# The second expert product turned round: 128 tokens of g held in the array, 512 columns of w_out streamed, the odd half blocks of two chunks joined

## The chip, the cores and the metric

The kernel runs on one core of a Trainium2 chip. The metric is the device time of one execution in microseconds (us). The reported time is a median of several runs; a profiled execution of the same kernel gives the trace, whose span runs from the first to the last instruction.

## What is computed

The reference is attention with a top-32 mask over 4 batches, 8 heads, 576 tokens and 64 columns a head, followed by a gated product of experts on 2304 tokens. Cut to what matters:

```python
scores = q @ k.T / 8                                  # per batch and head
mask = scores >= (32nd largest of each row)
attn = softmax(where(mask, scores, -1e9))
x = (attn @ v), heads side by side                    # 2304 x 512
a = x @ w_a; b = x @ w_b                              # 512 -> 1536
return (a * b) @ w_out                                # 1536 -> 512
```

The last line is the product that is changed. The letter g stands for a * b below.

## The kernel before

**Chunks and tiles.** The 576 tokens of each batch are cut into a chunk of 256 (`LO`) and one of 320 (`HI`). There are eight chunks, numbered 0 to 7 in the order of the work; their lengths are 256, 320, 256, 320, 256, 320, 320, 256. Attention goes through a chunk by four pairs of heads and, within a pair, by tiles of 64 tokens: 16 tiles for a chunk of 256, 20 for one of 320, 144 in all. For a tile, TensorE makes the scores (L430), VectorE finds the largest 32 of every row in rounds of MAX8 and MATCH_REPLACE8 (L458, L460), ScalarE, GpSimd or VectorE mask and exponentiate, TensorE transposes (L512). After the last tile of a pair, `av` multiplies by v (L540) and splits the result x into a high and a low part, `xh` and `xl` (L543, L544). A chunk's x is complete when the `xl` of its fourth pair is written.

**Experts.** `up(c, j, which)` (j from 0 to 11, which 0 or 1 for w_a and w_b) adds up 12 matmuls in a PSUM buffer of the tag `mm` (L570 to L572: high by high, high by low, low by high, four times). It needs the whole x of its chunk. The copy of the first product (L579) is multiplied by the second (L584, or L587 and L588 in chunks 0 and 1); g is split into `gh` (L589, ScalarE) and `gl` (L590, GpSimd), buffers that hold all twelve j of one chunk, one of each. `down(c, m)` makes the second product for 128 of the 512 output columns: per j three matmuls, L600 to L602, that hold 128 columns of w_out (`fin[j]`) in the array and stream the chunk's 256 or 320 tokens of gh or gl. Four blocks m, each of 36 matmuls, make a chunk. A block ends in a ScalarE copy out of PSUM (L606) and a store on SP's queue (L607) into an output that lies by columns of w_out, and which the host turns round at the end.

**The order of the work.** Every operation is enlisted in a `Plan` with its engine, its estimated cost, a key, and what it reads and writes. `Plan.order` simulates the engines and writes the order out: each engine, when it is free, takes the operation with the lowest key that is ready and for which a buffer is free. Attention has the keys 0 and up (some of it lower), the experts 1000 and up; what is equal goes by the order of enlisting. There are two `mm` buffers, which `up`, `down` and `av` share. Only while none of them is held, and TensorE would be idle, the plan puts in fillers: matmuls with zeros (L288). In the order of enlisting all ups of a chunk stand ahead of its downs. Each unit of `down` waits in the plan for all twelve gh and gl of its chunk:

```python
for j in range(NJ):
    pe(3 * n, lambda j=j: product(j), [(fin[j], 0), (fin[j], 1)] + [(y, k) for y in (gh, gl) for k in range(NJ)], [ps], num=3)
```

The weights come to the kernel in another format and are converted in the first 213 us (`convert`: L384 to L392), w_out last, j from 0 to 11. The ups of chunk 0 run over the j from 7 to 11 and then from 0 to 6; those of odd chunks after chunk 1 run over the j downward, so that the last ones are the small j. From tile 36 on (`COUPLED`) the scores of two tiles are made together, and the first copies and minima of the odd one get a key that is lower by `SOON`.

Of the kernel before, what the change touches and what calls it, by code (L numbers as in the profile page):

```python
# [8 lines left out]
FT = mybir.dt.float32  # L9
FR = mybir.dt.float32r  # L10
# [9 lines left out]
LOW = -3.0e38  # L20
LO, HI = 256, 320
W_BUFS = 8
COUPLED, SOON = 36, 2.5
KEEP = 1
GRP = 2

# [5 lines left out]
CONV_BIG = 4  # L32
# [219 lines left out]
def attn_moe(ctx: ExitStack, tc, qT, kT, v, wa, wb, wo, out):  # L252
# [19 lines left out]

    chunks = [(b, *x) for b in range(B) for x in ([(0, LO), (LO, HI)] if b < B - 1 else [(LO, HI), (0, LO)])]
    pairs = [(c, p) for c in range(len(chunks)) for p in range(NP)]
    tiles = []
    for c, p in pairs:
# [11 lines left out]
    def buf(shape, dtype, tag, bufs, pool=work):  # L290
        return Buf(pool, shape, dtype, tag, bufs)
# [53 lines left out]
    def convert(j, i):  # L345

        src = wo[j] if i == 2 else (wa, wb)[i][j].rearrange("p k e -> p (k e)")  # L350
        n = 2 * NJ + j if i == 2 else 2 * j + i
        if i == 2 and j in CONV_AWAY:
            raw, both = [buf([128, 1024], U4, "w", W_BUFS) for _ in range(2)]
            tmp, low = Part(both, 0, 512), Part(both, 512, 512)
            plan.enlist(raw, both)
        elif n < CONV_FIRST and n % CONV_BIG == CONV_BIG - 1:
            big = buf([128, 3840], U4, ("gh", "gl")[n // CONV_BIG % 2], 1)
            raw, tmp, low = [Part(big, *x) for x in ((0, 1024), (1024, 512), (1536, 512))]
        else:
            while i == 2 and len(listed) + 1 + 2 * sum(x not in CONV_AWAY for x in range(len(listed), j + 1)) > NJ:  # L360
                plan.enlist(fin[len(listed)])
                listed.append(fin[len(listed)])
            raw, both = [buf([128, 1024], U4, "wo", NJ, const) for _ in range(2)]
            tmp, low = Part(both, 0, 512), Part(both, 512, 512)
            plan.enlist(raw, both)
        first = [PR[0]["kr"], PR[0]["qr"]]
        dma(524e3, lambda: nc.sync.dma_start(raw[:, :], src.bitcast(U4)), [], [raw], after=first)
        if i == 2:
            w = fin[j]
            if j == NJ - 1:  # L370
                plan.enlist(*fin)
        else:
            w = buf([128, 2, 4, 128], FR, "w", W_BUFS)

        def word(t):
            return raw[:, :].rearrange("p (n t) -> p n t", t=2)[:, :, t]

        def part(k):
            return w[:, k] if i == 2 else w[:, k].rearrange("p k e -> p (k e)")

        def f(x):
            return x[:, :].bitcast(FT)

        act(512, lambda: nc.scalar.activation(f(tmp), word(1).bitcast(FT), AF.Relu, scale=2.0 ** -116), [raw], [tmp])  # L384
        act(512, lambda: nc.scalar.activation(f(low), word(1).bitcast(FT), AF.Relu, scale=-2.0 ** -84), [raw], [low])
        pool(512, lambda: nc.gpsimd.tensor_tensor(f(tmp), f(tmp), f(low), OP.add), [low], [tmp])
        act(512, lambda: nc.scalar.activation(low[:, :], word(0), AF.Copy, scale=2.0 ** -29 * (1 - 2.0 ** -13),  # L387
                                              bias=7.5 * 2.0 ** -13 - 0.5), [raw], [low])
        dve(0, lambda: vec.scalar_tensor_tensor(tmp[:, :], tmp[:, :], 3, low[:, :], op0=OP.logical_shift_left,
                                                op1=OP.bitwise_or), [low], [tmp], 0.6, port=True)  # L390
        act(512, lambda: nc.scalar.activation(part(0), f(tmp), AF.Copy), [tmp], [(w, 0)])
        pool(512, lambda: nc.gpsimd.tensor_tensor(part(1), f(tmp), part(0).bitcast(FT), OP.subtract), [tmp, (w, 0)], [(w, 1)])  # L392
        if i < 2:
            dma(524e3, lambda: move(wab_d[j][i], w.ap), [(w, 0), (w, 1)], [("wd", j, i)])
        return w
# [149 lines left out]
             [xf, (xh, p)], [(xl, p)])  # L545


    G, A, O = {}, {}, {}

    kept = {}  # L550

    def up(c, j, which, last=False):
        n = chunks[c][2]
        xh, xl = X[c]
        if (c, j, which) in direct:
            w = direct.pop((c, j, which))
            wt = [(w, 0), (w, 1)]
        elif (j, which) in kept:
            w = kept.pop((j, which))
            wt = [w]  # L560
        else:
            w = buf([128, 2, 4, 128], FR, "w", W_BUFS)
            wt = [w]
            dma(524e3, lambda: move(w.ap, wab_d[j][which]), [("wd", j, which)], [w])
        if last and c + 1 < len(chunks):
            kept[j, which] = w
        ps = mm_tile()

        def product(kb):
            mm(ps[:, :n], w[:, 0, kb, :], xh[:, kb, :n], start=(kb == 0), stop=False)  # L570
            mm(ps[:, :n], w[:, 0, kb, :], xl[:, kb, :n], start=False, stop=False)  # L571
            mm(ps[:, :n], w[:, 1, kb, :], xh[:, kb, :n], start=False, stop=(kb == 3))  # L572
        for kb in range(4):
            pe(3 * n, lambda kb=kb: product(kb), wt + [(y, k) for y in (xh, xl) for k in range(NP)], [ps], num=3)
        if which == 0:
            if c not in G:
                G[c] = (buf([128, NJ, HI], FR, "gh", 1), buf([128, NJ, HI], FR, "gl", 1))
            a = A[0] = buf([128, HI], FT, "a", 2)
            act(n, lambda: nc.scalar.activation(a[:, :n], ps[:, :n], AF.Copy, scale=UNIT), [ps], [a], ps=True, k=URGENT)  # L579
            return  # L580
        gh, gl = G[c]
        a = A[0]
        if c >= POOL_PRODUCT:
            dve(n, lambda: vec.scalar_tensor_tensor(a[:, :n], ps[:, :n], UNIT, a[:, :n], op0=OP.mult, op1=OP.mult), [ps], [a], k=URGENT)  # L584
        else:
            y = buf([128, HI], FT, "b", 1)
            act(n, lambda: nc.scalar.activation(y[:, :n], ps[:, :n], AF.Copy, scale=UNIT), [ps], [y], ps=True, k=URGENT)  # L587
            pool(n, lambda: nc.gpsimd.tensor_tensor(a[:, :n], a[:, :n], y[:, :n], OP.mult), [y], [a])  # L588
        act(n, lambda: nc.scalar.activation(gh[:, j, :n], a[:, :n], AF.Copy), [a], [(gh, j)], k=URGENT)  # L589
        pool(n, lambda: nc.gpsimd.tensor_tensor(gl[:, j, :n], a[:, :n], gh[:, j, :n].bitcast(FT), OP.subtract),  # L590
             [a, (gh, j)], [(gl, j)])

    def down(c, m):
        b, t0, n = chunks[c]
        gh, gl = G[c]
        ps = mm_tile()
        ms = slice(128 * m, 128 * m + 128)

        def product(j):
            mm(ps[:, :n], fin[j][:, 0, ms], gh[:, j, :n], start=(j == 0), stop=False)  # L600
            mm(ps[:, :n], fin[j][:, 0, ms], gl[:, j, :n], start=False, stop=False)  # L601
            mm(ps[:, :n], fin[j][:, 1, ms], gh[:, j, :n], start=False, stop=(j == NJ - 1))  # L602
        for j in range(NJ):
            pe(3 * n, lambda j=j: product(j), [(fin[j], 0), (fin[j], 1)] + [(y, k) for y in (gh, gl) for k in range(NJ)], [ps], num=3)
        o = buf([128, HI], FT, "b", 1)
        act(n, lambda: nc.scalar.activation(o[:, :n], ps[:, :n], AF.Copy, scale=UNIT), [ps], [o], ps=True, k=URGENT)  # L606
        dma(512 * n, lambda: nc.sync.dma_start(out[ms, b * S + t0:b * S + t0 + n], o[:, :n]), [o], [])  # L607


    key[0] = -1  # L610
# [3 lines left out]
    for i, t in enumerate(tiles):  # L614
# [38 lines left out]
                for which in range(2):  # L653
                    up(c, j, which, n >= NJ - KEEP)
        key[0] = EXPERTS + c
        for m in range(4):
            down(c, m)


    low, one = buf([128, 3], FT, "low", 1), buf([1, 1], FT, "one", 1)  # L660
# [18 lines left out]
def general(tc, qT, kT, v, wab, wo, ident, out):  # L679
# [7 lines left out]
    with (tc.tile_pool(name="gd", bufs=1, space=bass.MemoryType.DRAM) as dram, tc.tile_pool(name="ga", bufs=2) as sb,  # L687
# [46 lines left out]
        with tc.For_i(0, B, 1) as b:  # L734
            for g in range(2):
# [5 lines left out]
                for j in range(len(wo)):  # L741
                    ab = []
                    for i in range(2):
                        w = sb.tile([128, 2, 4, 128], FR, name="gw")
                        nc.sync.dma_start(w.bitcast(FT), wab[j][i].bitcast(FT))
                        p = ps.tile([128, HS], FT, name="gmm", bufs=2)
                        for kb in range(4):
                            mm(p, w[:, 0, kb, :], xh[:, kb], start=(kb == 0), stop=False)
                            mm(p, w[:, 0, kb, :], xl[:, kb], start=False, stop=False)
# [3 lines left out]
                    nc.vector.tensor_tensor(ab[0], ab[0], ab[1], OP.mult)  # L753
                    nc.scalar.activation(gh[:, j], ab[0], AF.Copy)
                    nc.gpsimd.tensor_tensor(gl[:, j], ab[0], gh[:, j].bitcast(FT), OP.subtract)
                for m in range(4):
                    ms = slice(128 * m, 128 * m + 128)
                    p = ps.tile([128, HS], FT, name="gmm", bufs=2)
                    for j in range(len(wo)):
                        mm(p, wo[j][:, 0, ms], gh[:, j], start=(j == 0), stop=False)  # L760
                        mm(p, wo[j][:, 0, ms], gl[:, j], start=False, stop=False)
                        mm(p, wo[j][:, 1, ms], gh[:, j], start=False, stop=(j == len(wo) - 1))
                    o = sb.tile([128, HS], FT, name="go")
                    nc.scalar.activation(o, p, AF.Copy, scale=UNIT)
                    nc.sync.dma_start(out[ms, ds(b * S + g * HS, HS)], o)


def layout(q, k, v, wa, wb, wo):
# [29 lines left out]
```

## Time and profile before

| | us |
|---|---|
| time, median of 3 runs | 854.4 |
| the 3 runs | 851.25, 854.4, 855.22 |
| profiled execution, its own time | 850.72 |
| its span | 849.0 |
| PE busy in the span | 796.8 (94%) |
| DVE busy | 695.2 (82%) |
| ACT busy | 595.1 (70%) |
| POOL busy | 406.2 (48%) |
| mean granted clock of PE, share of full speed | 0.988 |

PE is TensorE, PEld its weight loads, DVE VectorE, ACT ScalarE, POOL GpSimd, SP the engine that issues the transfers. A matmul's record runs to its modelled end, so the records of matmuls that follow each other overlap; the distance between two starts is what a matmul costs in a stream. A name such as L600 is a line of the kernel. The execution's own time is 1.72 us above its span.

### The profile page before, as it was taken

Reading aid. Unit: us, or ns where it says so; the run is one execution under the profiler, and the core shown is the slowest. Engines: PE = TensorE matmul, PEld = TensorE weight load, DVE = VectorE, ACT = ScalarE, POOL = GpSimd, SP = SyncE. Lnnn points to the kernel's source line nnn. Section 1 sums busy time; section 2 is a strip of 40 time slices with the busy share of each in tenths; the row PEclk is TensorE's granted clock in tenths of the full one; section 3 lists DMA queues with packets and bytes.
Section 4 is the critical chain, followed back from the end, with each engine's and each line's share of the span. In section 5 each row is a group of like instructions: output and inputs, shape, how many; then the busy total and the mean of one; then the engine's idle time right before and its main releaser. Section 6 shows DMA issues by size and latency. Waiting matters only on the chain.

```text
span 849.0 us, 18522 instructions
## 1 busy us (share of the span) xinstructions
PE 796.8 (94%) x6358; PEld 658.0 (77%) x6358; DVE 695.2 (82%) x2240; ACT 595.1 (70%) x1404; POOL 406.2 (48%) x541
## 2 busy tenths in 40 slices
PE   3787889899999999999999999999999999999997
PEld 1444457666888887888888888888888888999997
DVE  4898898988999999999999999999999999710010
ACT  4899988999687777777767777777777777621220
POOL 2677766976357753444444543345344443420120
PEclk8999999999999999999999999999999999999999
DMA  6778748865357732586247741685347721673540
GB/s 204 274 236 274 248 159 285 279 190 173 113 163 237 230 118 60 173 278 211 68 145 232 228 158 61 195 259 191 88 158 225 234 82 39 207 257 122 186 179 29
DMA packets 75430, 153.87 MB, mean 181 GB/s; under 512 B 7232, under 2 KB 46144, under 8 KB 75328
## 3 DMA queue, kind: packets, MB, share of 16 engines
q1 hardware_dynamic: 75328, 152.60, 55.8%
q8 instruction: 53, 0.87, 0.4%
q14 instruction: 49, 0.40, 0.2%
HBM read 135.27 MB, written 17.30 MB: 180 GB/s over the span
## 4 chain that ended last, share of the span: by engine, by line
PE 73%; ACT 11%; DVE 4%; POOL 4%; DMA 3%; issue 2%; SPq 2%; POOLq 0%; DVEq 0%; ACTq 0%
PE mm L570 11%; PE mm L571 10%; PE mm L572 10%; PE tp L512 8%; PE mm L540 8%; PE s L430 8%; PE mm L600 6%; PE mm L601 6%; PE mm L602 6%; ACT p L492 2%; DMA wo<-wa 2%; ACT r L485 1%; DVE mx L460 1%; DVE top L458 1%; ACT wo L387 1%
## 5 line engine op out<-in xcount | busy, mean ns | idle before, releaser
L570 PE MATMUL mm<-xh,w 128*128 128x256 f32 (+1 forms) x768 | 238.0, 310 | 1.0 <-ACT a L579 1.0
L572 PE MATMUL mm<-xh,w 128*128 128x256 f32 (+1 forms) x768 | 227.3, 296 | 0.0
L571 PE MATMUL mm<-xl,w 128*128 128x256 f32 (+1 forms) x768 | 227.2, 296 | 0.0
L458 DVE MAX8 top<-mx 128x8 f32<-128x296 f32 x432 | 187.3, 457 | 1.5
L570 PEld LDWEIGHTS mm<-xh,w 128*128 128x128 f32 x768 | 145.1, 189 | 18.6 <-issue 12.3
L571 PEld LDWEIGHTS mm<-xl,w 128*128 128x128 f32 x768 | 145.4, 189 | 0.0
L572 PEld LDWEIGHTS mm<-xh,w 128*128 128x128 f32 x768 | 144.8, 188 | 0.0
L517 ACT ACTIVATE pt<-tp 128x640 f32<-128x640 f32 x144 | 101.0, 701 | 56.7 <-PE tp L512 55.8
L590 POOL TENSOR_TENSOR gl<-a,gh 128x256 fp32r<-128x256 f32 (+1 forms) x96 | 79.3, 826 | 123.0 <-ACT gh L589 118.9
L460 DVE MATCH_REPLACE8 mx<-top,mx 128x296 f32<-128x296 f32 x288 | 128.7, 450 | 0.0
L499 POOL TENSOR_SCALAR p<-p,sm 128x576 f32<-128x576 f32 x97 | 74.2, 765 | 95.2 <-DVE sm L495 94.8
L600 PE MATMUL mm<-gh,wo 128*128 128x256 f32 (+1 forms) x384 | 119.0, 310 | 0.3 <-ACT b L606 0.2
L512 PE MATMUL tp<-ident,p 128*128 128x128 f32 x720 | 106.3, 279 | 8.3 <-POOL p L499 4.3
L601 PE MATMUL mm<-gl,wo 128*128 128x256 f32 (+1 forms) x384 | 113.6, 296 | 0.4 <-POOL gl L590 0.4
L602 PE MATMUL mm<-gh,wo 128*128 128x256 f32 (+1 forms) x384 | 113.6, 296 | 0.0
L430 PE MATMUL s<-kr,qr 64*64 64x288 f32 x1152 | 92.3, 424 | 20.1 <-ACT p L492 14.1
L512 PEld LDWEIGHTS tp<-ident,p 128*128 128x128 f32 x720 | 83.1, 142 | 25.9 <-POOL p L499 9.8
L584 DVE SCALAR_TENSOR_TENSOR a<-mm,a 128x256 f32<-128x256 f32 (+1 forms) x72 | 32.9, 456 | 85.3 <-PE mm L572 83.7
L475 POOL TENSOR_TENSOR p<-sb,p 128x576 f32<-128x576 f32 x55 | 78.4, 1426 | 43.2 <-ACT p L474 32.4
L540 PE MATMUL mm<-pt,vr 128*64 128x256 f32 (+1 forms) x640 | 84.7, 411 | 0.6 <-ACT pt L517 0.6
L600 PEld LDWEIGHTS mm<-gh,wo 128*128 128x128 f32 x384 | 72.6, 189 | 9.7 <-issue 7.8
L589 ACT ACTIVATE gh<-a 128x256 fp32r<-128x256 f32 (+1 forms) x96 | 42.4, 441 | 50.4 <-DVE a L584 47.2
(87 smaller groups left out, 1534.1 us busy)
## 6 DMA issues: line engine op xcount, KB each, us to landing
w<-wd SPq DMA_DIRECT2D x168, 512.0 KB, 4.4
wd<-w SPq DMA_DIRECT2D x24, 512.0 KB, 3.6
kr<-kT SPq DMA_DIRECT2D x64, 144.0 KB, 3.1
vr<-v SPq DMA_DIRECT2D x32, 256.0 KB, 3.1
wo<-wa SPq DMA_DIRECT2D x12, 512.0 KB, 5.1
qr<-qT SPq DMA_DIRECT2D x32, 160.0 KB, 3.3
wo<-wb SPq DMA_DIRECT2D x9, 512.0 KB, 5.1
qr<-qT SPq DMA_DIRECT2D x32, 128.0 KB, 3.4
```

Of the source, the lines that this page charges most:

```text
L430: mm(s[rows, g, 0:HS], qr[on, h, t["off"]:t["off"] + 64], kr[on, h, :], start=True, stop=True)
L458: dve(HS + 8, lambda r=r: vec.max(eight(r), mx[:, g]), [(mx, g, 0), (mx, g, 1)], [tk[r]], 0.393)
L460: dve(HS + 8, lambda r=r: vec.match_replace(mx[:, g], eight(r), mx[:, g], LOW), [tk[r]], [(mx, g, 0), (mx, g, 1)], 0.453)
L512: nc.tensor.transpose(tp[:, kb, :], pf[:, k0:k0 + 128], ident)
L517: act(640, lambda: nc.scalar.activation(turned[:, :, :, t["off"]:t["off"] + 64], tp.ap.rearrange("p k (h q) -> p k h q", h=2), AF.Copy), [ ...
L540: mm(ps[e, :n], vr[:, kb, e], turned[:, kb, h, :n], start=(kb == 0), stop=(kb == 4))
L570: mm(ps[:, :n], w[:, 0, kb, :], xh[:, kb, :n], start=(kb == 0), stop=False)
L571: mm(ps[:, :n], w[:, 0, kb, :], xl[:, kb, :n], start=False, stop=False)
L572: mm(ps[:, :n], w[:, 1, kb, :], xh[:, kb, :n], start=False, stop=(kb == 3))
L600: mm(ps[:, :n], fin[j][:, 0, ms], gh[:, j, :n], start=(j == 0), stop=False)
L601: mm(ps[:, :n], fin[j][:, 0, ms], gl[:, j, :n], start=False, stop=False)
L602: mm(ps[:, :n], fin[j][:, 1, ms], gh[:, j, :n], start=False, stop=(j == NJ - 1))
```

## The change

Each block of the second product now holds 128 tokens of gh or gl in the array and streams the 512 columns of a row block of w_out. The result of a block is 128 tokens by 512 columns, so the output lies by tokens and the host turns nothing round. A chunk of 320 tokens is two and a half blocks: the chunks are put in such an order that the two of 320 of neighbouring batches follow each other (256, 320, 320, 256, and the same again), and such a pair shares gh and gl, now 384 columns wide. The second chunk of a pair writes its g from column 64 on; the first 64 columns keep the first chunk's tokens 0 to 63. The first chunk's down takes its columns 64 to 319 in two blocks, the second one's takes all 384 in three, the first of which ends in two stores. A unit of the plan waits for the gh and gl of its own j alone, and the j are taken in the order in which the ups have made them (`turn`). The buffer b of the copies is 512 columns wide instead of 320, and `SOON` goes from 2.5 to 1.5. The path `general`, which runs only if the top-32 search falls short, is changed in the same way.

```diff
-COUPLED, SOON = 36, 2.5
+COUPLED, SOON = 36, 1.5
...
-    chunks = [(b, *x) for b in range(B) for x in ([(0, LO), (LO, HI)] if b < B - 1 else [(LO, HI), (0, LO)])]
+    chunks = [(b, *x) for b in range(B) for x in ([(0, HI), (HI, LO)] if b % 2 else [(0, LO), (LO, HI)])]
...
-            big = buf([128, 3840], U4, ("gh", "gl")[n // CONV_BIG % 2], 1)
+            big = buf([128, 4608], U4, ("gh", "gl")[n // CONV_BIG % 2], 1)
...
-    G, A, O = {}, {}, {}
+    G, A, turn = {}, {}, [[] for _ in chunks]
...
-                G[c] = (buf([128, NJ, HI], FR, "gh", 1), buf([128, NJ, HI], FR, "gl", 1))
+                G[c] = *[buf([128, NJ, HI + 64], FR, x, 1) for x in ("gh", "gl")], 0
+                if n == HI:
+                    G[c + 1] = *G[c][:2], 64
...
-        gh, gl = G[c]
-        a = A[0]
+        gh, gl, at = G[c]
+        on, a = slice(at, at + n), A[0]
+        if j not in turn[c]:
+            turn[c].append(j)
...
-            y = buf([128, HI], FT, "b", 1)
+            y = buf([128, 512], FT, "b", 1)
...
-        act(n, lambda: nc.scalar.activation(gh[:, j, :n], a[:, :n], AF.Copy), [a], [(gh, j)], k=URGENT)
-        pool(n, lambda: nc.gpsimd.tensor_tensor(gl[:, j, :n], a[:, :n], gh[:, j, :n].bitcast(FT), OP.subtract),
+        act(n, lambda: nc.scalar.activation(gh[:, j, on], a[:, :n], AF.Copy), [a], [(gh, j)], k=URGENT)
+        pool(n, lambda: nc.gpsimd.tensor_tensor(gl[:, j, on], a[:, :n], gh[:, j, on].bitcast(FT), OP.subtract),
              [a, (gh, j)], [(gl, j)])
 
-    def down(c, m):
+    def down(c, x):
         b, t0, n = chunks[c]
-        gh, gl = G[c]
+        gh, gl, at = G[c]
         ps = mm_tile()
-        ms = slice(128 * m, 128 * m + 128)
+        on = slice(x, x + 128)
 
         def product(j):
-            mm(ps[:, :n], fin[j][:, 0, ms], gh[:, j, :n], start=(j == 0), stop=False)
-            mm(ps[:, :n], fin[j][:, 0, ms], gl[:, j, :n], start=False, stop=False)
-            mm(ps[:, :n], fin[j][:, 1, ms], gh[:, j, :n], start=False, stop=(j == NJ - 1))
-        for j in range(NJ):
-            pe(3 * n, lambda j=j: product(j), [(fin[j], 0), (fin[j], 1)] + [(y, k) for y in (gh, gl) for k in range(NJ)], [ps], num=3)
-        o = buf([128, HI], FT, "b", 1)
-        act(n, lambda: nc.scalar.activation(o[:, :n], ps[:, :n], AF.Copy, scale=UNIT), [ps], [o], ps=True, k=URGENT)
-        dma(512 * n, lambda: nc.sync.dma_start(out[ms, b * S + t0:b * S + t0 + n], o[:, :n]), [o], [])
+            mm(ps.ap, gh[:, j, on], fin[j][:, 0], start=(j == turn[c][0]), stop=False)
+            mm(ps.ap, gh[:, j, on], fin[j][:, 1], start=False, stop=False)
+            mm(ps.ap, gl[:, j, on], fin[j][:, 0], start=False, stop=(j == turn[c][-1]))
+        for j in turn[c]:
+            pe(3 * 512, lambda j=j: product(j), [(fin[j], 0), (fin[j], 1), (gh, j), (gl, j)], [ps], num=3)
+        o = buf([128, 512], FT, "b", 1)
+        act(512, lambda: nc.scalar.activation(o.ap, ps.ap, AF.Copy, scale=UNIT), [ps], [o], ps=True, k=URGENT)
+        to = b * S + t0 + x - at
+
+        def store():
+            if x >= at:
+                nc.sync.dma_start(out[to:to + 128], o.ap)
+                return
+            nc.sync.dma_start(out[to + 64:to + 128], o[64:128])
+            b_, t_, _ = chunks[c - 1]
+            nc.sync.dma_start(out[b_ * S + t_:b_ * S + t_ + 64], o[0:64])
+        dma(262e3, store, [o], [], 2 if x < at else 1)
...
-        for m in range(4):
-            down(c, m)
+        n, at = chunks[c][2], G[c][2]
+        for x in range(n % 128 if not at else 0, at + n, 128):
+            down(c, x)
```

## Rows read from the trace of the kernel before

**Rows 1.** Busy time by stretch: start:end, length, each engine's busy time, clock, DMA share.

```profile
core 0: us, PE busy (x) PEld busy (x) DVE busy (x) ACT busy (x) POOL busy (x), PEclk, DMA share, GB/s
0.00:100.00 100.00, 69.16 (x490) 38.35 (x491) 81.17 (x232) 82.19 (x184) 62.54 (x72) 0.93 0.73 243
100.00:200.00 100.00, 88.51 (x695) 64.52 (x694) 89.11 (x256) 90.02 (x223) 73.76 (x85) 0.98 0.72 239
240.00:740.00 500.00, 497.16 (x4070) 423.81 (x4069) 479.42 (x1617) 372.99 (x882) 233.56 (x336) 1.00 0.54 169
740.00:849.00 109.00, 102.87 (x778) 100.43 (x776) 9.08 (x21) 21.12 (x50) 17.34 (x22) 0.99 0.46 157
```

**Rows 2.** The same view for the fillers of L288 alone.

```profile
100.00:200.00 100.00, 17.74 (x99) 8.76 (x97) 0.98 0.72 239
200.00:240.00 40.00, 1.74 (x9) 0.88 (x9) 1.00 0.33 99
240.00:740.00 500.00, 1.15 (x5) 0.41 (x5) 1.00 0.54 169
```

**Rows 3.** Timeline of POOL, L544: fourth xl of chunks 1, 2, 3, 6, 7.

```profile
236.07 0.89 POOL L544 TENSOR_TENSOR xl<-xf,xh 128x320 fp32r<-128x320 f32 x1
...
309.27 0.73 POOL L544 TENSOR_TENSOR xl<-xf,xh 128x256 fp32r<-128x256 f32 x1
...
404.44 0.87 POOL L544 TENSOR_TENSOR xl<-xf,xh 128x320 fp32r<-128x320 f32 x1
...
675.33 0.88 POOL L544 TENSOR_TENSOR xl<-xf,xh 128x320 fp32r<-128x320 f32 x1
...
747.14 0.74 POOL L544 TENSOR_TENSOR xl<-xf,xh 128x256 fp32r<-128x256 f32 x1 [4.47 <-ACT xh L543]
```

**Rows 4.** Timeline of ACT, L606: last copy of a down, chunks 0, 1, 6.

```profile
236.90 0.38 ACT L606 ACTIVATE b<-mm 128x256 f32<-128x256 f32 x1 [0.35 <-PE mm L602]
...
342.40 0.44 ACT L606 ACTIVATE b<-mm 128x320 f32<-128x320 f32 x1 [0.40 <-PE mm L602]
...
792.88 0.44 ACT L606 ACTIVATE b<-mm 128x320 f32<-128x320 f32 x1 [4.84 <-PE mm L602]
```

**Rows 5.** Timeline of PE: chunk 6's down from its 38th matmul, chunk 7's ups.

```profile
776.95 0.31 PE L601 MATMUL mm<-gl,wo 128*128 128x320 f32 x1
...
792.64 0.28 PE L570 MATMUL mm<-xh,w 128*128 128x256 f32 x1
...
824.19 0.28 PE L572 MATMUL mm<-xh,w 128*128 128x256 f32 x1
```

**Rows 6.** Matmul groups by line and form: count, busy us, mean ns.

```profile
L600 PE MATMUL mm<-gh,wo 128*128 128x320 f32 x192 | 62.1, 323 | 0.2 <-ACT b L606 0.2
...
L600 PE MATMUL mm<-gh,wo 128*128 128x256 f32 x192 | 56.9, 296 | 0.1
```

**Rows 7.** Timeline of POOL: the last halves of w_out, j = 9 and 11.

```profile
207.60 1.26 POOL L392 TENSOR_TENSOR wo<-wo 128x512 fp32r<-128x512 f32 x1
...
211.28 1.28 POOL L392 TENSOR_TENSOR wo<-w,wo 128x512 fp32r<-128x512 f32 x1
```

**Rows 8.** Timelines of POOL and PE: from chunk 7's ups to its down.

```profile
825.53 0.72 POOL L590 TENSOR_TENSOR gl<-a,gh 128x256 fp32r<-128x256 f32 x1 [2.13 <-ACT gh L589]
...
824.32 1.04 PE L288 MATMUL mm<-still,nident 128*128 128x256 bf16 x4
825.51 0.38 PE L600 MATMUL mm<-gh,wo 128*128 128x256 f32 x1
826.31 0.38 PE L601 MATMUL mm<-gl,wo 128*128 128x256 f32 x1 [0.42 <-POOL gl L590]
826.53 0.28 PE L602 MATMUL mm<-gh,wo 128*128 128x256 f32 x1
```

**Rows 9.** Timeline of all engines at the end of the span.

```profile
843.45 0.28 PE L602 MATMUL mm<-gh,wo 128*128 128x256 f32 x1
843.81 0.38 ACT L606 ACTIVATE b<-mm 128x256 f32<-128x256 f32 x1 [3.93 <-PE mm L602]
844.22 0.33 SPq L607 DMA_DIRECT2D out<-b  x1
```

**Rows 10.** Transfers: count, KB each, median us from issue to landing.

```profile
wd<-w SPq DMA_DIRECT2D x24, 512.0 KB, 3.6
...
vr<-v SPq DMA_DIRECT2D x32, 256.0 KB, 3.1
...
out<-b SPq DMA_DIRECT2D x16, 128.0 KB, 1.7
```

More of the change, by code (lines that the diff above doesn't have):

```diff
@@ L745, in general @@
                         nc.sync.dma_start(w.bitcast(FT), wab[j][i].bitcast(FT))
-                        p = ps.tile([128, HS], FT, name="gmm", bufs=2)
+                        p = ps.tile([128, 512], FT, name="gmm", bufs=2)[:, 0:HS]
                         for kb in range(4):
@@ L755, in general @@
                     nc.gpsimd.tensor_tensor(gl[:, j], ab[0], gh[:, j].bitcast(FT), OP.subtract)
-                for m in range(4):
-                    ms = slice(128 * m, 128 * m + 128)
-                    p = ps.tile([128, HS], FT, name="gmm", bufs=2)
+                for x in range(0, HS, 128):
+                    m = min(128, HS - x)
+                    p = ps.tile([128, 512], FT, name="gmm", bufs=2)
                     for j in range(len(wo)):
[L760 to L765, printed above, removed]
+                        for k, (g_, w) in enumerate(((gh, 0), (gh, 1), (gl, 0))):
+                            mm(p[:m], g_[:, j, x:x + m], wo[j][:, w], start=(j + k == 0), stop=(j == len(wo) - 1 and k == 2))
+                    o = sb.tile([128, 512], FT, name="go")
+                    nc.scalar.activation(o[:m], p[:m], AF.Copy, scale=UNIT)
+                    nc.sync.dma_start(out[ds(b * S + g * HS + x, m)], o[:m])
 def layout(q, k, v, wa, wb, wo):
@@ L792 @@
             for n, a in arrays.items()]
-    o = nc.dram_tensor("out", (H * D, B * S), FT, kind="ExternalOutput").ap()
+    o = nc.dram_tensor("out", (B * S, H * D), FT, kind="ExternalOutput").ap()
     with tile.TileContext(nc) as tc:
@@ L796 @@
     r = run_bass_kernel_spmd(nc, [arrays], core_ids=[0])
-    return np.ascontiguousarray(r.results[0]["out"].T)
+    return np.ascontiguousarray(r.results[0]["out"])
```

## The prediction

> **What bounds the kernel now.** I read the busy time by stretch first. It shows three stages [rows 1]. Up to 200 us TensorE is busy 69 and 89 us of each 100, and of the second of these 17.7 us are fillers [rows 2]: there attention and the conversion of the weights set the pace. From 240 to 740 TensorE is busy 497.2 of 500 us with 1.15 us of fillers, and VectorE 479.4: both are nearly full. From 740 on VectorE has 9 us of work and TensorE 102.9 of 109. The granted clock is 1.00 from 240 on, and 0.99 in the last stretch: the level of 2.4 GHz.
>
> Two engines at 96% and 99% leave open which of them sets the end, so I looked for what TensorE has in hand. The fourth xl of a chunk opens its experts. Chunk 1's comes at 236.07 [rows 3], when chunk 0's down has just ended (its last copy is at 236.90 [rows 4]): there TensorE has nothing in stock. Chunk 2's comes at 309.27, but chunk 1's down ends only at 342.4, so 32 us of work lie ready. Chunk 6's comes at 675.33 and chunk 7's at 747.14, and chunk 6's down ends at 792.88 [rows 3, 4]: the stock has grown to 45 us. From 237 us on TensorE always has expert work to put between the pieces of attention. Whatever its work after 237 us shrinks by, the end comes earlier by, as long as the stock doesn't run out. The same saving before 237 us only makes it wait for chunk 1's x.
>
> **Streaming: the columns stay, the count falls.** Before, 576 matmuls stream 256 columns and 576 stream 320 (192 of each form on each of three lines [rows 6]): 331,776 columns. After, the chunks of 256 have 2 blocks of 36 matmuls, the chunks 1 and 5 have 2, the chunks 2 and 6 have 3: 18 blocks, 648 matmuls of 512 columns, again 331,776. So the gain is what a matmul costs beside its columns, times 504.
>
> That cost is in the stream at the end [rows 5]. From 776.95 to 792.64 us lie 107 steps with 320 columns: 146.6 ns each. From 792.64 to 824.19 lie 263 steps with 256 columns: 120.0 ns. The 64 columns between them cost 26.7 ns, 0.417 ns a column, and each matmul has 13.2 ns more than its columns. No row shows 512 columns. I take the line through the two lengths: 512 x 0.417 + 13.2 = 226.7 ns. The second product then takes 648 x 0.2267 = 146.9 us instead of 576 x 0.1200 + 576 x 0.1466 = 153.6, which is 6.7 us less. The bounds: with none of the 13.2 ns left it is 648 x 0.2135 = 138.3 us (15.3 less); if the cost grew with the length, at the 320 columns' 0.458 ns a column, 152.0 us (1.6 less). The line is the nearest to both rows.
>
> The Trainium skill speaks against a gain of this size: its page "TensorE: Matmul & The Clock Gate", in the section "Wait — 56ns, not 53.3ns?", puts the fixed cost of a matmul in a warm stream at about 2.5 ns beside its columns. By that, 504 fewer matmuls would give 1.3 us, an estimate from the page. The trace does not agree: it has 13.2 ns at 256 and at 320 columns [rows 5], and I go by it.
>
> Of the 504, 72 are chunk 0's, before 237 us: 0.95 us that I don't count. The other 432 give **5.7 us**.
>
> **Chunk 0's down** now takes j = 7 to 11 first, and w_out is converted upward: j = 9 is complete at 208.9 us, j = 11 at 212.6 [rows 7]. The old order could do all but the last few j of its first block by then. At 212.6 the new one has 8 j of its first block and at most 12 of its second to do, 20 x 0.68 = 13.6 us; the old one has about 40 x 0.36 = 14.4 us to do and is through at 236.9 with attention in between. So it ends just in time for chunk 1's x. I take nothing, between a gain of 1 us and a loss of 5 (when both blocks hold the two mm buffers while they wait for j = 9 to 11, and the av in that stretch has none).
>
> **The wait before the last down.** Chunk 7's ups run j downward, its down upward, so the first product wants the g that is made last. The stream of ups ends at 824.32. The third matmul of the down would start at 824.56 in an unbroken stream; it starts at 826.53, since the last gl runs from 825.53 to 826.25 [rows 8]. With a unit that waits for its own j, in the order of the ups, the last j comes 11 x 0.68 = 7.5 us after the first: the **2.0 us** go. In the chunks before, the stock covers this wait, and nothing is to be had.
>
> **The end.** The last copy grows from 256 to 512 columns. The two lengths take 0.38 and 0.44 us [rows 4], so 0.94 ns a column and 0.62 us: 0.24 more. The last store has 256 KB instead of 128. The 128 KB land in 1.7 us; loads of 256 KB take 3.1 among other traffic, and stores of 512 KB 3.6 [rows 10]. Between 128 and 512 KB lies 2.3 us, 0.6 more, with bounds of 0 and 1.4. Together **0.8 us** late; all of it is on the path, as nothing follows the store but the end of the program [rows 9].
>
> **What costs nothing.** The copies L606 fall from 32 to 18 and from about 13 to 11 us of ScalarE, which is busy 373 of 500 us [rows 1]; if that cover were gone they would be worth 2 us. The stores fall from 32 to 20 issues, so the weight loads behind them on SP's queue stand behind fewer waits. The lower SOON shifts which tile's copies go first on ScalarE and VectorE, and the sums there stay. A unit of three matmuls grows from 0.36 or 0.44 to 0.68 us, and a piece of attention that becomes ready inside one waits 0.12 to 0.16 us longer on average. That lies in TensorE's own order and costs it no work, as long as the stock lasts. A third of chunk 6's down is work moved from chunk 5's; for an engine that is never out of work that is nothing.
>
> **The stock at chunk 2** is the thin place. Chunk 2 now has 20 tiles. At the pace of its 16 (309.27 - 236.07 = 73.2 us) they take 91.5 us, at the pace of chunk 3's 20 they take 95.2 [rows 3], so its x is there at 328.5 to 332. Chunk 1's experts cost 288 x 0.1466 = 42.2 us of ups and 21.1 of down, 63.3 in the 105 us from 237 to 342: a share of 0.60. The down falls to 72 x 0.2267 = 16.3, so it ends 4.8 / 0.60 = 8 us earlier, at 334. Two to six microseconds of stock are left of 32. I take no loss here.
>
> **Sum.** -5.7 - 2.0 + 0.8 = -6.9 us. The profiled execution goes from 850.72 to 843.8 us, its span from 849.0 to 842.1. The median of the runs is 3.7 us above the profiled execution; the same difference on it gives 854.4 - 6.9 = **847.5 us**, 0.8% less. Half a per cent, 4.3 us, is about what this kernel's runs (851.25 to 855.22) can tell from no change; so faster is below 850.1 and slower above 858.7.
>
> **The rivals.** *The fixed cost does not come back with 512 columns*: the swap of the weights is hidden behind a longer stream. Then chunks 1 to 7 save 136.3 - 576 x 0.2135 = 13.3 us instead of 5.7: 839.9 us. Against it: at 320 columns it is as large as at 256. The page named above would leave 2.5 ns of it here, an estimate of 841.3 us.
>
> *TensorE runs out of work at chunk 2, or chunk 0's down ends late*: each microsecond that chunk 2's x comes after chunk 1's down, or that chunk 0's down ends after 237, comes off the gain one for one. For it: the thin stock, and the 40 us in which chunk 1 arrived exactly at the end of chunk 0's down. With 3 to 7 us lost it is 850.5 to 854.5 us. If VectorE set the pace up to 740, only the tail would change: chunk 6's down +3.4 (108 x 0.2267 against 144 x 0.1466), chunk 7's -1.0, the wait -2.0, the end +0.8, which is 855.6 us.
>
> *Slower*: attention's pace on chunk 2 falls, because its scores and transposes stand behind longer units and the odd tiles' copies go later. The place is 237 to 334 us, the price 1 us for each that the x comes after 334; it decides from 345 on (more than 11.2 us late), when a tile takes 5.4 us instead of 4.6 to 4.8. It would give 859 to 862 us. Against it: 0.16 us on each of two or three pieces of a tile, and only during downs, makes 20 tiles 2 to 4 us longer at most.
>
> **Chances.** The forecast, 844 to 850 us: 0.60. The larger gain: 0.10. The stock runs out or the early down is late, within half a per cent: 0.22. Slower: 0.08. So faster 0.70, same 0.22, slower 0.08. The range reaches from the larger gain's 840 to 854: left out are the slower case, the upper end of the case before it, and what is below the larger gain.
>
> **What would show it.** In the last down the starts should be 227 ns apart (214 to 216 for the larger gain, 235 if the cost grows with the length). No filler and no idle time should lie between the last up and the last down. Fillers between 240 and 740 should stay near 1 us; more of them around 328 to 340 us mean that the stock ran out. Chunk 0's last copy should be near 237. The last store should land 0.6 us later after its issue than before. The prediction is wrong above all if TensorE's idle time after 237 us grows by more than 3 us.

## The result, and the profile after

The changed kernel takes 844.26 us (median of 4 runs, 840.68 to 844.59) against 854.81 us for the kernel before beside it: a ratio of 0.9875, interval 0.9837 to 0.9914. Measured a second time it took 843.32 against 851.48 us: 0.9900 (0.9877 to 0.9924). It is faster by about 1%; 847.5 was forecast. The profiled execution took 844.30 us, and its span is 842.3 (forecast 842.1). One run of those reported below is left out of its median: 988.28 us of the kernel with chunk 0 upward, at a granted clock of 0.75, where the five others lie between 839.37 and 842.77.

The busy time by stretch of the changed kernel (columns as in [rows 1]):

```profile
200.00:240.00 40.00, 35.40 (x237) 22.84 (x237) 36.53 (x120) 29.28 (x70) 20.49 (x28) 0.96 0.36 110
240.00:740.00 500.00, 498.70 (x3807) 407.41 (x3806) 482.36 (x1619) 372.83 (x875) 232.32 (x339) 1.00 0.55 173
740.00:842.30 102.30, 97.33 (x623) 88.69 (x622) 9.22 (x25) 21.77 (x49) 16.96 (x21) 1.00 0.45 148
...
205.00:212.00 7.00, 3.19 (x27) 1.72 (x25) 6.63 (x21) 6.10 (x16) 3.54 (x4) 0.91 0.02 6
212.00:216.00 4.00, 3.79 (x20) 2.22 (x18) 3.79 (x12) 2.86 (x7) 3.07 (x4) 0.72 0.25 82
```

From 240 to 740 TensorE has some 260 matmuls fewer and is as full as before (498.7 against 497.2 us). The span ends 6.7 us earlier. What is new are the last two rows: from 205 to 212 us TensorE works 3.19 of 7 us, and from 212 to 216 its granted clock is 0.72, between the two levels of 1.2 and 2.4 GHz. In the kernel before, the same two stretches are:

```profile
205.00:212.00 7.00, 6.13 (x50) 4.00 (x47) 5.48 (x17) 6.04 (x15) 4.58 (x7) 1.00 0.22 60
212.00:216.00 4.00, 4.00 (x37) 3.39 (x36) 3.93 (x14) 2.85 (x8) 2.12 (x3) 1.00 0.79 253
```

The same view for the fillers of L288 alone has none left where [rows 2] had nine and five:

```profile
200.00:240.00 40.00, 0.00 (x0) 0.00 (x0) 0.96 0.36 110
240.00:740.00 500.00, 0.00 (x0) 0.00 (x0) 1.00 0.55 173
```

**Where the time went.** I cut the span at two matmuls that both kernels have: the first up of chunk 1 and the last matmul of all. Between them I took the distance from each TensorE instruction's start to the next one's and added these up by kind.

| us | before | after | change |
|---|---|---|---|
| start of chunk 1's first up | 237.59 | 242.33 | +4.73 |
| from there to the last matmul's start | 605.85 | 594.61 | -11.24 |
| of it, down | 144.1 | 137.1 | -7.0 |
| of it, fillers | 2.3 | 0 | -2.3 |
| of it, transposes | 54.2 | 52.3 | -1.8 |
| of it, up, scores, av | 405.3 | 405.1 | -0.2 |
| last matmul's start to the end of the span | 5.56 | 5.34 | -0.22 |
| span | 849.0 | 842.3 | -6.7 |

The rows by kind hold whatever idle time stands behind an instruction of that kind. So the stretch behind chunk 1's first up gained more than the forecast's 6.9 us, and 4.7 us of that were lost ahead of it. The second profiled execution of the changed kernel has 594.61 us in the middle again, to the hundredth; its executions differ ahead of that stretch and behind it.

**The late start.** TensorE's timeline, changed kernel, from chunk 0's down to chunk 1's first up (start, us, line, operation, tiles, shape, count, and in brackets the idle time before it and what ended it):

```profile
204.22 0.71 PE L512 MATMUL tp<-ident,p 128*128 128x128 f32 x5
204.86 0.72 PE L430 MATMUL s<-kr,qr 64*64 64x288 f32 x8
206.78 0.74 PE L512 MATMUL tp<-ident,p 128*128 128x128 f32 x5 [1.20 <-POOL p L499]
207.78 0.40 PE L490 MATMUL s<-r,nident 128*128 128x288 bf16 x2 [0.26 <-ACT r L485]
209.73 0.72 PE L430 MATMUL s<-kr,qr 64*64 64x288 f32 x8 [1.55 <-ACT p L492]
211.24 1.33 PE L512 MATMUL tp<-ident,p 128*128 128x128 f32 x5 [0.79 <-POOL p L499]
212.22 0.78 PE L604 MATMUL mm<-wo,gh 128*128 128x512 f32 x1
...
226.21 2.91 PE L540 MATMUL mm<-pt,vr 128*64 128x320 f32 x20
...
241.64 0.39 PE L606 MATMUL mm<-wo,gl 128*128 128x512 f32 x1
...
242.33 0.40 PE L570 MATMUL mm<-xh,w 128*128 128x320 f32 x1
```

Until 204.2 the two blocks of chunk 0's down have done their j = 7 and 8. Then no matmul of a down runs for 8 us. Both `mm` buffers are held, so the av of chunk 1's third pair starts at 226.21. In the kernel before it starts at 204.44:

```profile
204.44 2.91 PE L540 MATMUL mm<-pt,vr 128*64 128x320 f32 x20
```

GpSimd and ScalarE show, in the changed kernel, when x and the buffers are ready:

```profile
236.26 0.89 POOL L544 TENSOR_TENSOR xl<-xf,xh 128x320 fp32r<-128x320 f32 x1 [1.00 <-ACT bias L462]
...
330.25 0.89 POOL L544 TENSOR_TENSOR xl<-xf,xh 128x320 fp32r<-128x320 f32 x1
```

```profile
242.42 0.58 ACT L610 ACTIVATE b<-mm 128x512 f32<-128x512 f32 x1
...
337.05 0.60 ACT L610 ACTIVATE b<-mm 128x512 f32<-128x512 f32 x1 [0.45 <-PE mm L606]
```

Chunk 1's x is there at 236.26 + 0.89 = 237.15 us, as before (236.96, [rows 3]); but chunk 0's last copy comes at 242.42 instead of 236.90 [rows 4]. Chunk 1's ups begin 5.2 us after their x; before, 0.6. The gap does not hang on when attention is done: it is 5.19 us in the second profiled execution and 5.47 and 5.18 in the two experiments below that keep this order and this wait (streams of 256, no joining), where x comes at 237.36, 234.07 and 238.36. At chunk 2 the stock holds: its x is ready at 331.1, chunk 1's last copy comes at 337.05.

**The tail.** TensorE's timeline from chunk 7's last up to the last matmul:

```profile
820.69 0.28 PE L572 MATMUL mm<-xh,w 128*128 128x256 f32 x1
820.81 0.40 PE L604 MATMUL mm<-wo,gh 128*128 128x512 f32 x1
...
836.94 0.39 PE L606 MATMUL mm<-wo,gl 128*128 128x512 f32 x1
```

The down follows the ups in one step, with neither the fillers nor the wait of [rows 8], although the last gl is made only from 822.03 on:

```profile
822.03 0.74 POOL L594 TENSOR_TENSOR gl<-a,gh 128x256 fp32r<-128x256 f32 x1 [2.14 <-ACT gh L593]
```

Its 71 steps take 16.13 us: 227.2 ns each, where the line through [rows 5] gave 226.7.

### The profile page after: what moved, and what is told of

It reads as the page before. It is cut to its first block, busy times and chain, and to the rows that moved or that the text cites. A ratio compares the mean times of both kernels' runs of the same rounds, so it can differ in the third digit from the quotient of the medians.

```text
span 842.3 us, 17408 instructions
## 1 busy us (share of the span) xinstructions
PE 788.7 (94%) x5828; PEld 621.3 (74%) x5828; DVE 696.7 (83%) x2240; ACT 594.2 (71%) x1390; POOL 404.2 (48%) x541
## 5 line engine op out<-in xcount | busy, mean ns | idle before, releaser
L571 PE MATMUL mm<-xl,w 128*128 128x256 f32 (+1 forms) x768 | 227.2, 296 | 0.0
L588 DVE SCALAR_TENSOR_TENSOR a<-mm,a 128x320 f32<-128x320 f32 (+1 forms) x72 | 32.8, 455 | 78.5 <-PE mm L572 76.5
L604 PE MATMUL mm<-wo,gh 128*128 128x512 f32 x216 | 90.0, 417 | 0.0
L606 PE MATMUL mm<-wo,gl 128*128 128x512 f32 x216 | 84.9, 393 | 0.0
L605 PE MATMUL mm<-wo,gh 128*128 128x512 f32 x216 | 84.8, 393 | 0.0
L430 PEld LDWEIGHTS s<-kr,qr 64*64 64x64 f32 x1152 | 36.6, 134 | 55.6 <-ACT p L492 23.2
L450 DVE TENSOR_TENSOR mn<-s,sb 128x288 f32<-128x288 f32 x144 | 64.0, 446 | 16.1 <-ACT sb L443 14.0
```

The source lines that it names most:

```text
L430: mm(s[rows, g, 0:HS], qr[on, h, t["off"]:t["off"] + 64], kr[on, h, :], start=True, stop=True)
L604: mm(ps.ap, gh[:, j, on], fin[j][:, 0], start=(j == turn[c][0]), stop=False)
L605: mm(ps.ap, gh[:, j, on], fin[j][:, 1], start=False, stop=False)
L606: mm(ps.ap, gl[:, j, on], fin[j][:, 0], start=False, stop=(j == turn[c][-1]))
```

## The experiments

The theory that was to be tested has two halves. *Behind 240 us* the gain is streaming's and the own j's, each by itself. *Ahead of it* the loss comes from the order of chunk 0's blocks, which open with j = 7 to 11 while w_out is converted from j = 0 upward (theory A); the rival B puts it down to the early start of blocks that wait only for their own j and hold both buffers. Below, "the middle" is the stretch from chunk 1's first up to the last matmul. The kernel before beside the first four took 852.5 us, beside the next four 851.48.

**Chunk 0 upward.** Chunk 0's blocks take the j upward, after all twelve g. (Upward with the wait for the own j alone was not run: w_out's small j are converted first, so both blocks could take both buffers while ups that need a buffer are still to come. So this edit changes both halves of the early down at once, and a later run takes them apart.)

```diff
+        turn[0].sort()
...
-            pe(..., [(fin[j], 0), (fin[j], 1), (gh, j), (gl, j)], [ps], num=3)
+            pe(..., [(fin[j], 0), (fin[j], 1)] + [(y, k) for y in (gh, gl) for k in ([j] if c else range(NJ))], [ps], num=3)
```

> The changed kernel, but chunk 0's down takes j from 0 to 11 again and waits for all twelve g, as before. Theory A: in the changed kernel chunk 0's down took j = 9 to 11 early and waited for w_out, ended at 242.4 us instead of 236.9, and each microsecond of that is lost. Then chunk 0's last copy comes back to 236 to 238 us and the span falls from 842.3 to 837 to 838.5. Rival B: the late start was not on the path, or what is won there is lost at chunk 2, whose x comes at 330 to 331 us while chunk 1's down would now end at about 332. Then the span stays at 841 to 843, and fillers or idle time stand around 330 us.

Measured: 841.3 us, ratio 0.9878 (0.9841 to 0.9915); span 838.2, in the 837 to 838.5 that were expected; chunk 1's first up at 237.84, the middle 595.14. The gap between x and the ups is 0.3 us. The loss lies in chunk 0's down, as expected. The ratio against the kernel before is that of the changed kernel, though, so whether it shows in the time took a direct comparison (below).

**Streams of 256 again.** Each matmul of 512 columns is cut in two of 256, with the same operand in the array.

```diff
-            mm(ps.ap, gh[:, j, on], fin[j][:, 0], ...)
...
+            for k, (g_, w) in enumerate(((gh, 0), (gh, 1), (gl, 0))):
+                for e in (slice(0, 256), slice(256, 512)):
+                    mm(ps[:, e], g_[:, j, on], fin[j][:, w, e], ...)
```

> The changed kernel, but every matmul of the second product is two of 256 columns, with the same weights loaded twice: 1296 matmuls instead of 648, the same columns. Theory A (13.2 ns for each matmul beside its columns): starts 120 ns apart in the last down, 648 x 13.2 = 8.6 us more, a span of 850.9. Rival B (2.5 ns, as the page on the clock gate has it): 1.6 us more, a span of 843.9. Rival C (it is the turned orientation and not the count that gains): no change, 842 to 843.

Measured: 849.18 us, ratio 0.9973 (0.9955 to 0.9991); the middle grows by 5.7 us to 600.34, less than theory A's 8.6 (7.6 of them in the middle) and far more than the 1.6 and 0 of its rivals. TensorE's timeline of its end:

```profile
838.32 0.40 PE L606 MATMUL mm<-wo,gl 128*128 128x256 f32 x2
838.56 0.64 PE L606 MATMUL mm<-wo,gh 128*128 128x256 f32 x4
839.04 0.40 PE L606 MATMUL mm<-wo,gl 128*128 128x256 f32 x2
839.28 0.64 PE L606 MATMUL mm<-wo,gh 128*128 128x256 f32 x4
839.76 0.40 PE L606 MATMUL mm<-wo,gl 128*128 128x256 f32 x2
```

From 838.32 to 839.76 lie 12 matmuls: 120.0 ns each, 240 for 512 columns against 227.2. So in the last down a matmul more costs 12.8 ns beside its columns, also when its operand is the one just used (the operand is loaded anew for each of the 1296). Between 240 and 740 us it costs less: there two halves take 2 x 119.8 = 239.6 ns and one matmul of 512 columns 230.4 (below), which by count gives 396 x 9.2 + 180 x 13.0 ns = 6.0 us, an estimate near the 5.7 measured. By the Trainium skill's page "TensorE: Matmul & The Clock Gate", section "Wait — 56ns, not 53.3ns?", a matmul's fixed cost is about 2.5 ns, and the middle would have grown by 576 x 2.5 ns = 1.4 us, an estimate from the page. The trace does not agree: 12.8 ns and 5.7 us.

**No joining.** Each chunk has its own gh and gl; a chunk of 320 has two full blocks and one of 64 tokens.

```diff
-                if n == HI:
-                    G[c + 1] = *G[c][:2], 64
...
+        r = min(128, n - x)
+        on = slice(x, x + r)
...
-        for x in range(n % 128 if not at else 0, at + n, 128):
+        for x in range(0, n, 128):
```

> The changed kernel, but the chunks of 320 are not joined: each has three blocks, of 128, 128 and 64 tokens, so 20 blocks and 720 matmuls. Theory A (a matmul costs its 512 columns however many of the array's columns hold tokens): 72 x 0.2267 = 16.3 us more, a span of about 858.6, slower than the kernel before. Rival B (a block of 64 tokens costs half, since half the array is idle): 8 us more, 850. Rival C (TensorE has time to spare): no change.

Measured: 858.69 us, ratio 1.0068 (1.0043 to 1.0093): slower than the kernel before. The middle is 610.61, 16.0 us more than in the changed kernel. Two blocks of 36 matmuls more at 0.2267 us are 16.3: with 64 tokens in the array the same 512 columns stream, and between 240 and 740 us such a matmul takes 229.9 ns in a run, one with 128 tokens 230.5. Turned round without the joining, the product loses more than it gains.

**The kernel before with the own j.** The other half alone: the product, the chunks' order and the columns as they were, but units that wait for their own j, in the order of the ups (chunk 0 upward after all twelve).

```diff
+        turn[0].sort()
+        for j in turn[c]:
-            pe(3 * n, ..., [(fin[j], 0), (fin[j], 1)] + [(y, k) for y in (gh, gl) for k in range(NJ)], [ps], num=3)
+            pe(3 * n, ..., [(fin[j], 0), (fin[j], 1)] + [(y, k) for y in (gh, gl) for k in ([j] if c else range(NJ))], [ps], num=3)
```

> The kernel before, with one part of the change alone: outside chunk 0 a unit of the second product waits for the gh and gl of its own j, and the j go in the order of the ups. Theory A: the wait of 2.0 us ahead of the last down goes, and the fillers of 1.1 us between chunk 2's ups and its down (397.8 to 399.5 us) go too, since they are the same wait where no stock covers it: a span of 845.5 to 846.3 instead of 849.0. Rival B: only the last one, 847.0. Rival C: the g would come too late in this order as well, 848.5 to 849.5.

Measured: 845.85 us, ratio 0.9930 (0.9904 to 0.9955); the middle 599.79 instead of 605.85. That is 6.1 us, about twice what was expected. Besides the wait at the last down (2.0 us, in which 1.2 of the 2.3 us of fillers stood), the other 1.1 us of fillers are gone, and so are two waits of TensorE, for attention and for a copy. They stand in TensorE's timeline of the kernel before:

```profile
333.00 0.31 PE L602 MATMUL mm<-gh,wo 128*128 128x320 f32 x1
334.89 0.77 PE L512 MATMUL tp<-ident,p 128*128 128x128 f32 x5 [1.57 <-ACT p L497]
...
381.70 0.39 PE L570 MATMUL mm<-xh,w 128*128 128x256 f32 x1 [1.03 <-ACT a L579]
...
397.76 0.61 PE L288 MATMUL mm<-still,nident 128*128 128x256 bf16 x2
398.44 0.77 PE L512 MATMUL tp<-ident,p 128*128 128x128 f32 x5
399.04 0.60 PE L288 MATMUL mm<-still,nident 128*128 128x256 bf16 x3
399.48 0.39 PE L600 MATMUL mm<-gh,wo 128*128 128x256 f32 x1
```

The last four rows are chunk 2's down waiting for its last g, with fillers in the gap. Chunk 3's x came only at 404.44 [rows 3], so at that moment there was no stock.

**The changed kernel again, and chunk 0 upward beside it.** Both in one measurement.

> The changed kernel itself, as the measure for the three others on this chip: 0.985 to 0.99 of the kernel before. In its own profile chunk 1's first up should again start 4 to 5 us later than in the kernel before (242.3 against 237.6).

> The first experiment's kernel again (chunk 0's down upward and after all twelve g), beside the changed kernel on one chip. Theory A: 3 to 5 us faster than the changed kernel, a ratio to the kernel before lower by 0.004 to 0.006. Rival B (the late chunk 0 costs nothing that can be timed): the same ratio within 0.002.

Measured: the changed kernel 843.32 us, ratio 0.9900 (0.9877 to 0.9924). Upward 840.94, ratio 0.9866 (0.9839 to 0.9893). The medians differ by 2.4 us, less than theory A's 3 to 5 and more than rival B's 0.002 of the time (1.7 us); the intervals overlap a little. Run by run they hardly do: the slowest of the five upward runs, 842.77, is above one of the changed kernel's six (842.60 to 845.10), and the other four are below all of them. What the trace shows is firm: in the same stretch of the upward kernel TensorE is never idle, and its clock stays at 1.00.

```profile
205.00:212.00 7.00, 7.00 (x47) 4.12 (x39) 6.76 (x22) 5.69 (x13) 4.17 (x5) 1.00 0.07 21
212.00:216.00 4.00, 4.00 (x29) 2.68 (x32) 2.80 (x10) 3.59 (x11) 4.00 (x6) 1.00 0.56 185
```

But at the end of it TensorE waits for x instead. The upward kernel's timeline, where the down is through before x (its last xl ends at 239.65):

```profile
235.73 0.40 PE L606 MATMUL mm<-wo,gl 128*128 128x512 f32 x1
...
237.79 1.68 PE L288 MATMUL mm<-still,nident 128*128 128x256 bf16 x10
239.45 0.74 PE L512 MATMUL tp<-ident,p 128*128 128x128 f32 x5
239.94 0.39 PE L570 MATMUL mm<-xh,w 128*128 128x320 f32 x1
```

In this execution attention came 2.5 us later than in the changed kernel's (237.15), which took half of the 4.9 us back. In the first experiment's execution of the same kernel it came at 237.55, 2.1 us earlier.

**SOON.** Chunk 0 upward, with `SOON` at 2.5 as before.

> The same as the kernel with chunk 0 upward, but SOON is 2.5 again as before the change. Theory A: SOON only shifts which tile's copies go first while TensorE is never out of work: no difference beyond 1.5 us. Rival B: the lower SOON is what took away the small waits of TensorE for the transposes (1.6 us at 334 us in the kernel before): 2 to 4 us slower.

Measured: 840.51 us, ratio 0.9861 (0.9833 to 0.9889); the middle 594.46 against 595.14. `SOON` makes no difference that can be measured.

**All twelve g.** The changed kernel with every chunk's j upward and every unit waiting for all twelve g, as in the kernel before: streaming and joining alone.

```diff
+        turn[c].sort()
...
-            pe(..., [(fin[j], 0), (fin[j], 1), (gh, j), (gl, j)], [ps], num=3)
+            pe(..., [(fin[j], 0), (fin[j], 1)] + [(y, k) for y in (gh, gl) for k in range(NJ)], [ps], num=3)
```

> The changed kernel with the old order: every unit of the second product waits for all twelve gh and gl, and j goes from 0 to 11 in all chunks. Streaming, join and SOON stay changed. Theory A (streaming 5.7 us and own j 6 us are separate gains, as the earlier experiment with own j alone has it): 5 to 6 us slower than the kernel with chunk 0 upward, a ratio to the kernel before of about 0.993 to 0.995. Rival B (the own j gains only the 2.0 us ahead of the last down, what else it moved was chance in the order): 2 us slower, 0.989 to 0.991.

Measured: 845.66 us, ratio 0.9931 (0.9908 to 0.9955); the middle 600.44, 5.3 us above the upward kernel. 2.1 us of fillers are back, and so is the wait at the last down:

```profile
817.54 0.28 PE L572 MATMUL mm<-xh,w 128*128 128x256 f32 x1
817.66 0.28 PE L288 MATMUL mm<-still,nident 128*128 128x256 bf16 x1
818.86 0.50 PE L604 MATMUL mm<-wo,gh 128*128 128x512 f32 x1 [0.91 <-ACT gh L593]
```

The two halves are about equal and add up: own j alone 6.1 us on the kernel before and 5.3 on the new product; streaming and joining alone 605.85 - 600.44 = 5.4 with all twelve g, and 599.79 - 595.14 = 4.7 with the own j.

**The order of chunk 0 alone.** j = 7 to 11 and then 0 to 6, as in the changed kernel, but after all twelve g (the second edit of the first experiment without the first): A against B.

> The changed kernel, but chunk 0's down waits for all twelve g, and keeps its order 7 to 11, then 0 to 6. It tells which half of the edit in the kernel with chunk 0 upward brings the 5 us back. Theory A (the order against the conversion of w_out): chunk 1's first up still starts 4 to 5.5 us after chunk 1's last xl, as in the changed kernel (5.2). Rival B (the units that start early and hold both mm buffers): it starts within 1 us of it, as in the kernel with chunk 0 upward (0.3).

Measured (one run): 848.97 us, the kernel before beside it 851.04. Chunk 1's first up starts at 238.63, 4.0 us after its last xl (233.77 + 0.87). So of the 5.2 us the order alone leaves 4.0, at the lower edge of A's range: A carries most of it, and at most 1.2 is the early start. The third av is held back here too, to 223.47 (205.51 in the first experiment's kernel). What this kernel does not have is the lower clock:

```profile
205.00:212.00 7.00, 5.02 (x32) 3.01 (x31) 6.76 (x21) 5.59 (x14) 3.83 (x5) 1.00 0.01 2
212.00:216.00 4.00, 4.00 (x29) 2.88 (x28) 3.86 (x12) 2.98 (x7) 2.42 (x3) 1.00 0.57 167
```

The wait that A names, for the converted w_out, stands in TensorE's timeline of this kernel:

```profile
208.46 0.71 PE L430 MATMUL s<-kr,qr 64*64 64x288 f32 x8 [1.25 <-ACT p L492]
...
210.33 0.50 PE L605 MATMUL mm<-wo,gh 128*128 128x512 f32 x1 [0.73 <-POOL wo L392]
```

The middle of this kernel is 602.63, 8.0 us above the changed kernel's with the same units and chunks behind chunk 0. TensorE's work there has not changed; it waits 5.4 us instead of 1.3, in pieces of at most 1.2 us scattered over the span (0.95 us for transposes at 509.70, 1.23 for scores at 602.06), and the remaining 3.9 were not taken apart. The plan has written another order from the small shift in chunk 0: behind chunk 1's first up TensorE's sequence differs from the seventh matmul on, while the two profiled executions of the changed kernel have one and the same. So some microseconds between two of these kernels can come from the order that the plan happens on, and the sizes above (5.3 and 6.1 us for the own j among them) carry that doubt.

## Why the prediction was right, and where it was not

| step | forecast, us | measured, us |
|---|---|---|
| 512 columns, chunks 1 to 7 | -5.7 | -4.2 |
| wait ahead of the last down | -2.0 | -2.0 |
| waits and the rest in the chunks before | 0 | about -5 |
| the end | +0.8 | -0.2 |
| chunk 0's down | 0 (-1 to +5) | +4.7 |
| sum, profiled execution | -6.9 | -6.7 (span), -6.4 (own time) |

**The sum is right to half a microsecond, and that is partly luck:** a gain of some 5 us that the forecast did not have and a loss of 4.7 that it held at nothing cancelled.

**Streaming** went by the mechanism named. In the last down the step is 227.2 ns. But of the steps inside runs of such matmuls, the 319 between 240 and 740 us have a mean of 230.4 ns, while those of 256 and 320 columns in the same stretch keep their 120 and 147. With 396 matmuls at 230.4 and 180 at 227.0 the chunks 1 to 7 take 132.1 us instead of 136.3: 4.2 us. The term was mis-sized by 1.5 us. The larger gain (213.5 ns) is excluded.

The rise goes with the place in a run. This run stands between scores and transposes (first, second, twelfth and last matmul):

```profile
684.61 0.50 PE L604 MATMUL mm<-wo,gh 128*128 128x512 f32 x1
684.96 0.40 PE L605 MATMUL mm<-wo,gh 128*128 128x512 f32 x1
...
687.28 0.39 PE L606 MATMUL mm<-wo,gl 128*128 128x512 f32 x1
...
688.64 0.39 PE L606 MATMUL mm<-wo,gl 128*128 128x512 f32 x1
```

From the second to the twelfth lie 232 ns a step, from there to the last 226.7. Over all runs the ten steps from the second matmul on have a mean of 231.4 ns between 240 and 740 us, and 229.3 after 740, where VectorE has 9 us of work; the later steps have 226.7 in both stretches. So the line was right for a long run, and the forecast left out that attention cuts the down into short ones.

**The last wait** went as worked out, 2.0 us. The sentence that failed is "In the chunks before, the stock covers this wait, and nothing is to be had". It took the stock of 32 us at chunk 2's x and of 45 at chunk 7's for the stock throughout. At the end of chunk 2, ahead of chunk 3's x, it was empty: fillers stood there in the trace of before, five of them in [rows 2], and they were read as a small number and not as the place of a wait. The own j on the kernel before is worth 6.1 us, of which the last wait is 2.0. Of the about 5 us elsewhere in the changed kernel, 1.1 are the other fillers and 1.5 idle time: 2.8 us before, nearly all of it in the two waits shown with the own j, and one wait of 1.30 in the changed kernel:

```profile
653.43 0.77 PE L512 MATMUL tp<-ident,p 128*128 128x128 f32 x5 [1.30 <-ACT p L497]
```

The remaining 2.4 us were not taken apart, and part of them can be chance in the order.

**Chunk 0's down** was costed at nothing with a bound of 5 and the right mechanism for that bound; it came out at 4.7. The step that failed is the comparison of work left at 212.6 us (13.6 against 14.4 us of down). Those numbers came true, but they count the down alone. Left out is that chunk 1's third av, 2.9 us of work, was also pushed behind 212, since both buffers were held, so that TensorE stood idle for 3.8 of the 7 us ahead of it, where it was idle for 0.9 before: 2.9 us. The clock fell too: 0.72 from 212 to 216, which is worth 0.28 x 4 = 1.1 us. Together that is an estimate of 4.0 of the 4.7 us. The second profiled execution divides it otherwise:

```profile
205.00:212.00 7.00, 3.71 (x28) 1.75 (x27) 6.55 (x22) 6.30 (x15) 3.33 (x4) 0.81 0.01 2
212.00:216.00 4.00, 4.00 (x16) 2.61 (x18) 3.79 (x13) 2.98 (x7) 3.26 (x4) 0.50 0.23 81
```

There it is 2.4 us of idle time more than before and 2.0 of clock, with the same gap behind x.

**The end.** The copy took 0.60 us (forecast 0.62) and stores of 256 KB landed in 2.0 (the median of 16; forecast 2.3, 128 KB took 1.7). Yet from the last store's issue to the end of the span passed 4.24 us, before 4.78: what follows a store varies by as much as was counted (from the last matmul to the end, 5.2 to 5.9 us over these kernels).

**The stock at chunk 2** was 5.9 us (331.14 to 337.05), where two to six were foreseen, and neither the changed kernel nor the upward one shows a filler there. Attention's pace did not fall: the slower rival has nothing for it.

**The median** came out 3.2 us below the forecast because the 3.7 us between the profiled execution and the median of before were carried over; after, the two are the same (844.30 and 844.26). So the offset was not a property of the change but where one execution fell among runs that differ by 4 us (851.25 to 855.56, and 840.68 to 844.59). The ratios 0.9875 and 0.9900 stand against a forecast 847.5 / 854.4 = 0.992.

**What the runs recommend:** the change with chunk 0's blocks upward, at 0.9866 and 0.9861 of the kernel before in one measurement, where the change itself is at 0.9900. By the single runs of that measurement it is better than the change, by 2 to 3 us; the intervals of the two ratios alone would not show it, and in the first measurements the ratios of the two were the same (0.9878 and 0.9875).

## What to carry to other kernels

Where an engine is full for 500 us, look at each filler and short wait by its place before saying that a stock covers it: the mean stock says nothing of the one chunk at which it is empty. When a unit is made longer or starts earlier, ask which buffers it holds while it waits and for whom, and let it take its inputs in the order in which they are made. Take what an instruction costs from runs as short as those in which it will stand. In a kernel whose order a planner writes out, a few microseconds can come from another order alone, so take the same edit on two kernels before giving it a price.

## What was not expected of the hardware

A matmul of this kind costs 13 to 14 ns beside its columns at 256, 320 and 512 columns (120.0, 146.6 and 226.7 ns a step in a long run), also when the same operand is loaded twice running. At 512 columns the ten steps from the second matmul of a run on cost some 5 ns more (231.4 ns between 240 and 740 us, against 226.7 for the steps behind them); at 256 and 320 columns they don't (119.4 and 146.2 in the kernel before). Busy engines alone are not what makes the difference, since the later steps keep 226.7 among them, and after 740 us the early ones still have 229.3; what the first steps wait for was not tried. An operand of 64 columns costs as much as one of 128 (229.9 against 230.5 ns). And a TensorE that was busy 3.19 us of 7, at a granted clock of 0.91, was granted 0.72 in the next 4 us, although it was busy in 3.79 of these; in the second execution it was 3.71 of 7 us at 0.81, and then 0.50 in 4 us in which it was busy throughout.
